# A decode kernel that streams 544 MB: seven small weight loads in one descriptor a partition instead of two, and a reordered last head

## The chip, the cores and the metric

The kernel runs on one core of one Trainium2 chip. The metric is the device time in microseconds (us), the median of several executions. A second number is used throughout: the *span*, from the first to the last of the program's own instructions in the trace. The device time is above the span, and how much above is called *outside* below.

The engines of the core have short names in the profile; in this kernel PE does matmuls (PEld is its loading of weights), DVE does elementwise work and reductions, ACT applies functions such as exp, POOL does next to nothing (0.9 us busy), and SP issues the loads. A load is described by *descriptors*, and here each descriptor became one *packet* (the change takes 7 x 128 descriptors away, and the page after has exactly 896 packets less), moved by one of the core's sixteen DMA engines. A load has *landed* when its last packet has arrived. The *granted clock* is the share of full speed that PE is allowed at a time; the clock records of the traces before and after hold only 1.00 and 0.50.

A ratio is the mean time of one kernel's fast runs over that of the kernel before in the same rounds, so it is not quite the ratio of the medians quoted beside it.

## The reference, cut to what matters

One token is decoded: 16 query heads share 8 key/value heads ("pairs" of query heads), with 65,536 cached tokens of 256 values each. The output is projected by `wo`, mixed with a small MLP branch and gated.

```
def _A_ref(x, k_cache, v_cache, wq, wo):          # Hq, Hkv, Sk, Dh = 16, 8, 65536, 256;  D = 448
    q = (x @ wq) ...
    scores = jnp.einsum("bhqd,bhkd->bhqk", q, k) * (Dh ** -0.5)
    p = _softmax(scores, axis=-1)
    o = jnp.einsum("bhqk,bhkd->bhqd", p, v)
    return o.reshape(B, Sq, Hq * Dh) @ wo
# return g * a + (1 - g) * b
```

K and V together are 537 MB. They must be read once, so the kernel is a stream with some arithmetic beside it. (The cut leaves out transposes and the repeating of K and V.)

## The kernel before

SP issues every load on one queue: for each of 32 steps a K load and a V load of 8 MB each (128 partitions of 64 KB), and at the first step of each of the eight pairs 448 KB of `wo`. The `wo` slice of a pair has 512 rows of 448 bf16 values. Partition p gets rows 2p and 2p+1 of each of the two query heads, which are two runs of 1792 bytes, hence two descriptors a partition:

```
    load(vbuf, A_v_cache, j, 0, NLATE if last else NV, 0, sem_v)
    if last:
        for (n0, n1), sem in zip(pieces, sem_vp):      # pieces = (96,112), (112,124), (124,128)
            load(vbuf, A_v_cache, j, n0, n1, 0, sem)
    if j % PPH == 0:
        g = j // PPH
        if g >= 1:
            eng.wait_ge(s_proj, g)
        eng.dma_start(wo_sb[:, :, :], A_wo[g * REP * DH:(g + 1) * REP * DH, :].rearrange(
                          "(h p j) n -> p h (j n)", h=REP, j=2)).then_inc(sem_wo, 16)
```

PE multiplies values by weights in *column groups*: four tokens share one bank, each in its own 32 rows. At a head change DVE copies the bank to `accs`, two selecting matmuls (`by_d`) bring the sums into columns, DVE divides by the denominators, and PE projects with `wo`. In the last head the last tokens are instead multiplied directly into columns (`late_values`), so that the copy (0.46 us in the timeline below) and the selecting matmuls (0.61 us) need not come after the last byte:

```
    some(0, NLATE).then_inc(s_early, 1)                # column groups, tokens 0 to 95
    ... else branch of the last step:
    def tail():
        late_values(*pieces[0])                        # tokens 96..111, directly
        pe.wait_ge(s_cp, H)                            # DVE has copied accs
        by_d(sps[:, 0, 0:2 * REP])                     # two selecting matmuls
        late_values(pieces[1][0], NV).then_inc(s_late, 1)   # tokens 112..127, directly
        pe.wait_ge(sem_wo, 16 * H)
        pe.wait_ge(s_oTn, H)
        project()
```

The softmax here doesn't subtract the row's maximum and nothing guards it: scores larger than these inputs give would overflow.

Of the kernel before, what the change touches and what calls it, by code (L numbers as in the profile page):

```python
# [8 lines left out]
ALU = mybir.AluOpType  # L9
# [3 lines left out]
def bass_gated_mix__gqa_block_cached__mixer_token_mlp__decode_kernel(  # L13
# [15 lines left out]
    f32 = mybir.dt.float32  # L29

    H = A_k_cache.shape[1]
    T = A_k_cache.shape[2]
    DH = A_k_cache.shape[3]
    DM = A_x.shape[-1]
    HQ = A_wq.shape[1] // DH
    REP = HQ // H
    F = B_w1.shape[1]
    FT = F // 128
    P = 128
# [11 lines left out]
    NV = BODY * NT  # L51
# [9 lines left out]



    NLATE = 96
    pieces = [(NLATE, 112), (112, 124), (124, NV)]


    NCG = 4
# [22 lines left out]
    with ctx:  # L91
        def sb(shape, dt, name):
            return ctx.enter_context(nc.sbuf_tensor(name, shape, dt))
# [17 lines left out]

        wo_sb = sb([P, REP, 2 * DM], bf16, "wo_sb")

        early = vbuf[:, :, :].rearrange("p n d -> p (n d)")
        early_f = vbuf_f[:, :, :].rearrange("p n d -> p (n d)")
        wq_a = early[:, 0:WF * NQ].rearrange("p (j n) -> p j n", j=WF)
# [26 lines left out]
        zrow = sb([1, NACC], bf16, "zrow")  # L143
        rden = sb([P, REP], f32, "rden")
        densum = sb([P, REP], f32, "densum")
        b2_b = sb([1, 1], bf16, "b2_b")
        stat = sb([1, 8], f32, "stat")
        statb = sb([1, 8], bf16, "statb")
# [65 lines left out]
        @block.sync  # L214
        def _(eng):
            eng.dma_start(wq_a.rearrange("p j n -> p (j n)"),  # L216
                          A_wq[0:WF * P, :].rearrange("(p j) n -> p (j n)", p=P)).then_inc(sem_wq, 16)
            eng.dma_start(wq_b, A_wq[WF * P:DM, :].rearrange("r (a n) -> (r a) n", a=2)  # L218
                          ).then_inc(sem_wq, 16)
            def load(dst, cache, j, n0, n1, at, sem):  # L220
                eng.dma_start(dst[:, at + n0:at + n1, :].rearrange("p n d -> p (n d)"), src(cache, j, n0, n1)  # L221
                              ).then_inc(sem, 16)

            for j in range(NP):
                last = j == NP - 1
                if j >= 1:
                    eng.wait_ge(sem_tr[NB - 1], BODY * (j - 1) + DC)
                if j == 0:
                    load(kring, A_k_cache, j, HV, NV, 0, sem_k)
                    load(kring, A_k_cache, j, 0, HV, 0, sem_kb)  # L230
                elif last:
                    load(kring, A_k_cache, j, 0, HV, HV, sem_k)
                    load(kring, A_k_cache, j, HV, NV, HV, sem_kb)
                else:
                    load(kring, A_k_cache, j, 0, NV, HV * (j % 2), sem_k)
                if j == 0:
                    eng.wait_ge(s_q, 1)
                    eng.wait_ge(s_hb, 1)
                else:
                    eng.wait_ge(sem_pv, j)  # L240
                load(vbuf, A_v_cache, j, 0, NLATE if last else NV, 0, sem_v)
                if last:
                    for (n0, n1), sem in zip(pieces, sem_vp):
                        load(vbuf, A_v_cache, j, n0, n1, 0, sem)
                if j % PPH == 0:
                    g = j // PPH
                    if g >= 1:
                        eng.wait_ge(s_proj, g)
                    eng.dma_start(wo_sb[:, :, :],
                                  A_wo[g * REP * DH:(g + 1) * REP * DH, :].rearrange(  # L250
                                      "(h p j) n -> p h (j n)", h=REP, j=2)).then_inc(sem_wo, 16)
            eng.wait_ge(s_fin, 1)
            eng.dma_start(out_ap, out_g[0:P:P // NCG, :]).then_inc(sem_out, 16)
            eng.wait_ge(sem_out, 16)
# [13 lines left out]
        def _(pe):  # L268
# [54 lines left out]
            def values(j, c0, u16):  # L323
                with pe.If(j == NP - 1):
                    spin(8)
                pe.wait_ge(sem_exp, c0 + (BODY + 2))
                for r in range(BODY):
                    pe.matmul(acc[:, DENC:SELC], ones_sq[:, :], pT[:, r, :],  # L328
                              start=False, stop=(r == BODY - 1), skip_group_check=True)

                def some(n0, n1):
                    pe.wait_ge(sem_v, u16)
                    for n in range(n0, n1):
                        r, nt = divmod(n, NT)
                        o = 32 * (n % 4)
                        ins = pe.matmul(acc[o:o + REP, 0:DH], pT[:, r, 2 * nt:2 * nt + 2], vbuf[:, n, :],  # L336
                                        start=False, stop=False, skip_group_check=True)
                    return ins

                some(0, NLATE).then_inc(s_early, 1)  # L340
                with pe.If(j < NP - 1):
                    some(NLATE, NV).then_inc(sem_pv, 1)
                with pe.Else():
                    tail()

            def piece_wait(n):
# [4 lines left out]
            def late_values(n0, n1):  # L351
                for n in range(n0, n1):
                    r, nt = divmod(n, NT)
                    piece_wait(n)
                    for dj in range(2):
                        ins = pe.matmul(sps[:, 0, dj * REP:(dj + 1) * REP], vbuf[:, n, dj:DH:2],  # L356
                                        pT[:, r, 2 * nt:2 * nt + 2], start=(n == NLATE and dj == 0),
                                        stop=(n == NV - 1), skip_group_check=True)
                return ins

            def by_d(dst):
                for dj in range(2):
                    ins = pe.matmul(dst[:, dj * REP:(dj + 1) * REP], accs[:, dj:DH:2], sel[:, :],
                                    start=False, stop=True, skip_group_check=True)
                return ins

            def clear(bank):
                pe.matmul(bank, ones_sq[0:1, :], zrow[0:1, 0:bank.shape[-1]], start=True, stop=True,
                          skip_group_check=True)

            def project():
                for hh in range(REP):
                    for dj in range(2):
                        j = dj * REP + hh
                        for q in range(NCG):
                            ins = pe.matmul(prj[32 * q:32 * q + 1, 0:WG], oTn[:, j:j + 1],  # L376
                                            wo_sb[:, hh, dj * DM + q * WG:dj * DM + (q + 1) * WG],
                                            start=False, stop=True, skip_group_check=True)
                ins.then_inc(s_proj, 1)


            def tail():
                late_values(*pieces[0])
                pe.wait_ge(s_cp, H)
                by_d(sps[:, 0, 0:2 * REP])
                late_values(pieces[1][0], NV).then_inc(s_late, 1)
                pe.wait_ge(sem_wo, 16 * H)
                pe.wait_ge(s_oTn, H)
                project()

            pe.sem_inc(sem_qk, 2)
            pe.wait_ge(sem_ident, 1)
# [34 lines left out]
            with nc.Fori(0, H, 1, engines=on, head_slot={pe.engine: 0}) as g:  # L427
                with nc.Fori(0, PPH, 1, engines=on, head_slot={pe.engine: 0}) as m:
                    j = pe.snap(g * PPH + m, min_val=0, max_val=NP - 1)
                    c0 = pe.snap(j * BODY, min_val=0, max_val=NC)  # L430
                    u16 = pe.snap(j * 16 + 16, min_val=16, max_val=16 * NP)
                    keys(c0, j, u16, pe.snap(x2_reg, min_val=0, max_val=NV))
                    values(j, c0, u16)
                    with pe.If(j < FT):
                        pe.wait_ge(s_pb, j + 1)
                        for q in range(NCG):
                            pe.matmul(prj[32 * q:32 * q + 1, WG:2 * WG], w2cur[:, :],
                                      gu[:, q * WG:(q + 1) * WG], start=False, stop=True, skip_group_check=True)
                    pe.reg_sub(x2_reg, NV, x2_reg)
                with pe.If(g < H - 1):  # L440
                    pe.wait_ge(s_cp, g + 1)
                    clear(acc[:, 0:NACC])
                    by_d(acc[:, SELC:NACC]).then_inc(s_sel, 1)
                    pe.wait_ge(sem_wo, pe.snap(g * 16 + 16, min_val=16, max_val=16 * H))
                    pe.wait_ge(s_oTn, g + 1)
                    project()

        @block.vector
        def _(vec):
# [107 lines left out]
            def finish_head(g):  # L557
                take(vec.snap(g * PPH + PPH, min_val=PPH, max_val=NP))
                vec.tensor_copy(qcur[:, :, :], qT[:, :, bass.ds(g * REP + REP, REP)])
                vec.drain()  # L560
                vec.wait_ge(s_sel, g + 1)
                by_head(acc[:, SELC:NACC])

            vec.wait_ge(s_q, 1)
            vec.tensor_copy(qT[:, :, :].rearrange("p a b -> p (a b)"), sps[:, 1, 0:2 * HQ])
# [23 lines left out]
            with nc.Fori(NC - NCPH, NC, BODY, engines=on) as c0:  # L589
                for k in range(BODY):  # L590
                    evacuate(k, c0 + k)
            take(NP, s_early)
            vec.wait_ge(s_late, 1)
            by_head(sps[:, 0, 0:2 * REP])
            vec.wait_ge(s_proj, H)
# [71 lines left out]
```

## Time and profile before

| | before |
|---|---|
| median of 3 runs | 1267.58 us (1267.54 to 1267.93) |
| span of the profiled run | 1265.7 us |
| busy: PE, ACT, DVE | 72%, 42%, 33% |
| DMA queue, share of 16 engines' span | 99.6% |
| last V piece has landed (trace's semaphore record) | 1262.00 us after the start |

First some lines of the page of the kernel before: the span, the busy time of the engines (with shares and instruction counts), the busy share of the DMA engines in 40 slices, their packets, the one data queue, and the shares of the chain of work that ended last.

```profile
span 1265.7 us, 38663 instructions
...
PE 911.9 (72%) x17040; PEld 861.1 (68%) x17041; DVE 418.2 (33%) x741; ACT 537.2 (42%) x786; POOL 0.9 (0%) x7
...
DMA  9999999999999999999999999999999999999998
...
DMA packets 12509, 544.39 MB, mean 430 GB/s; under 512 B 1360, under 2 KB 3410, under 8 KB 3794
...
q1 hardware_dynamic: 12408, 544.22, 99.6%
...
DMA 70%; PE 29%; issue 1%; SPq 0%; DVE 0%; ACT 0%; ACTq 0%
```

The DMA row is at 9 (90% or more) from the first slice to the last but one, and the queue's packets fill 99.6% of what sixteen engines have. So the queue does not run dry, and bytes and packets decide when the last byte lands. That the chain gives 29% to PE only says that a load is issued when PE has freed a buffer (the queue waited 31 times for the PE line L336 below, and 31 times for PE's reading of K); mostly 7 to 12 us of other loads are still queued at that moment (an estimate: K loads land 27.8 us after their issue and V loads 29.8 us in the median, and successive landings are 19.4 us apart, which leaves 8 and 10 us).

The queue's own waits before, by the line of the kernel that waits, what it waited for, the time in total, the number of waits and the longest:

```profile
SPq L221 <- PE acc L336: 531.3, 31, 23.7
...
SPq L249 <- PE prj L376: 13.0, 7, 1.9
```

The second line is the wait for the projection ahead of a `wo` load. It happens seven times and lasts 1.9 us at most.

The end of the timeline before. The columns are start in us, time in us, engine, line, operation, tiles, shapes and count; in brackets the idle time before and what ended it.

```profile
1257.11 2.79 PE L336 MATMUL acc<-vbuf,pT 128*2 128x256 bf16 x96 [0.72 <-DMA vbuf<-in_A_v_cache_dram]
...
1259.83 0.96 PE L356 MATMUL sps<-pT,vbuf 128*128 128x2 bf16 x32
1259.95 0.46 DVE L543 COPY accs<-acc 128x288 f32<-128x288 f32 x1 [6.80 <-PE acc L336]
...
1260.65 0.61 PE L363 MATMUL sps<-sel,accs 128*128 128x2 f32 x4
...
1261.45 0.95 PE L356 MATMUL sps<-pT,vbuf 128*128 128x2 bf16 x32 [0.19 <-DMA vbuf<-in_A_v_cache_dram]
1262.44 0.16 DVE L554 TENSOR_TENSOR oTn<-sps,rden 128x4 bf16<-128x4 f32 x1 [1.51 <-PE sps L356]
...
1262.75 0.54 PE L376 MATMUL prj<-wo_sb,oTn 128*1 128x112 bf16 x16 [0.35 <-DVE oTn L554]
1263.34 0.33 DVE L596 SCALAR_TENSOR_TENSOR out_g<-prj,bcast,run_g 128x112 bf16<-128x112 f32 x1 [0.74 <-PE prj L376]
```

The 96 tokens in column groups are followed by tokens 96 to 111 directly (L356), the copy on DVE (L543), the two selecting matmuls (L363), the last 16 tokens (L356 again, at 1261.45), the division (L554), the projection (L376), and the output step (L596). The 12-token piece landed at 1261.40 and the 4-token piece at 1262.00.

One more line, the window over the projection before: window, its length, then busy us (and count) of PE, weight loads, DVE, ACT and POOL, the granted clock of PE, the DMA share and GB/s.

```profile
1262.60:1263.30 0.70, 0.54 (x16) 0.31 (x16) 0.00 (x1) 0.00 (x0) 0.00 (x0) 0.50 0.00 0
```

The clock granted to PE was 0.50 there. The clock's records say that it fell at 1262.58 us. The records in this trace stand on a grid of 3.41 us.

### The profile page before, as it was taken

The numbers are of one execution on the slowest core, as the hardware profiler recorded it, in microseconds if no ns is written. First come the engines' busy times: TensorE is split into PE (matmuls) and PEld (weight loads), VectorE is DVE, ScalarE is ACT, GpSimd is POOL, SyncE is SP. The second block draws the span as 40 slices with busy tenths as digits, with TensorE's granted clock in tenths as the row PEclk, the third lists the DMA queues.
The fourth block names the chain that finished last, engine by engine and source line by source line (L and its number), as shares of the span: only waits on it lengthen the run. The fifth ranks groups of instructions, "written<-read, shape, count | busy, mean of one in ns | idle before, by whom it ended". The sixth has DMA issues, their size and how long they took to land.

```text
span 1265.7 us, 38663 instructions
## 1 busy us (share of the span) xinstructions
PE 911.9 (72%) x17040; PEld 861.1 (68%) x17041; DVE 418.2 (33%) x741; ACT 537.2 (42%) x786; POOL 0.9 (0%) x7
## 2 busy tenths in 40 slices
PE   2876668766778666787666876768867678666698
PEld 2766668766677666686665876657766578665687
DVE  2433334333344233343222332223322233331233
ACT  1543335533355333454333553335543245432455
POOL 0000000000000000000000000000000000000000
PEclk9888789788898788888788888789887788887989
DMA  9999999999999999999999999999999999999998
GB/s 412 428 429 437 431 435 433 433 431 437 431 433 435 431 433 437 429 435 435 431 433 433 433 435 435 431 427 439 433 435 435 425 433 439 433 435 429 431 426 353
DMA packets 12509, 544.39 MB, mean 430 GB/s; under 512 B 1360, under 2 KB 3410, under 8 KB 3794
## 3 DMA queue, kind: packets, MB, share of 16 engines
q1 hardware_dynamic: 12408, 544.22, 99.6%
q8 instruction: 8, 0.13, 0.0%
q10 hardware_dynamic: 90, 0.01, 0.0%
q14 instruction: 3, 0.02, 0.0%
HBM read 544.22 MB, written 0.00 MB: 430 GB/s over the span
## 4 chain that ended last, share of the span: by engine, by line
DMA 70%; PE 29%; issue 1%; SPq 0%; DVE 0%; ACT 0%; ACTq 0%
DMA kring<-in_A_k_cache_dram 68%; PE kst L284 24%; PE sps L304 4%; DMA vbuf<-in_A_v_cache_dram 2%; PE acc L336 0%; PE sps L356 0%; SPq L221 0%; PE prj L376 0%; SPq L218 0%; SPq L216 0%; PE acc L328 0%; DVE out_g L596 0%; ACT pT L621 0%; DVE oTn L554 0%; ACTq L621 0%
## 5 line engine op out<-in xcount | busy, mean ns | idle before, releaser
L284 PE MATMUL kst<-ident,kring 128*128 128x128 f32 x4096 | 560.9, 298 | 313.2 <-DMA kring<-in_A_k_cache_dram 301.1
L632 ACT ACTIVATE ktT<-kst 128x1024 bf16<-128x1024 bf16 x512 | 499.4, 1021 | 669.1 <-PE kst L284 668.8
L284 PEld LDWEIGHTS kst<-ident,kring 128*128 128x128 f32 x4096 | 511.1, 155 | 322.9 <-issue 320.7
L538 DVE COPY ktT<-kst 128x1024 bf16<-128x1024 bf16 x512 | 354.3, 692 | 771.5 <-PE kst L284 748.2
L304 PEld LDWEIGHTS sps<-qcur,ktT 128*128 128x128 bf16 x8192 | 237.7, 96 | 4.9 <-issue 2.4
L304 PE MATMUL sps<-qcur,ktT 128*128 128x2 bf16 x8192 | 236.7, 163 | 2.0 <-issue 2.0
L336 PE MATMUL acc<-vbuf,pT 128*2 128x256 bf16 x4064 | 145.1, 312 | 2.3 <-issue 1.6
L336 PEld LDWEIGHTS acc<-vbuf,pT 128*2 128x2 bf16 x4064 | 107.3, 95 | 31.6 <-issue 2.1
L621 ACT ACTIVATE pT<-sps 128x32 f32 x256 | 52.2, 204 | 17.0 <-PE sps L304 17.0
L328 PE MATMUL acc<-pT,ones_sq 128*128 128x32 bf16 x256 | 11.7, 178 | 12.2 <-ACT pT L621 12.2
L328 PEld LDWEIGHTS acc<-pT,ones_sq 128*128 128x128 bf16 x256 | 8.6, 96 | 15.2 <-ACT pT L621 14.9
L543 DVE COPY accs<-acc 128x288 f32<-128x288 f32 x8 | 3.7, 458 | 39.6 <-PE acc L336 39.6
L638 ACT ACTIVATE z_b<-z_b 128x448 bf16<-128x448 bf16 x14 | 8.1, 576 | 20.5 <-DVE z_b L525 20.5
L400 PE MATMUL acc<-vbuf 42*128 42x42 bf16 x1 | 0.2, 214 | 8.3 <-DMA b_b<-in_B_b_dram 8.3
L517 DVE TENSOR_TENSOR wtmp<-u_b 128x448 bf16<-128x448 bf16 x14 | 5.5, 393 | 1.0
L523 DVE TENSOR_TENSOR z_b<-u_b,wtmp 128x448 bf16<-128x448 bf16 x14 | 5.5, 393 | 1.0
L519 DVE TENSOR_TENSOR z_b<-wtmp,u_b 128x448 bf16<-128x448 bf16 x14 | 5.5, 393 | 1.0
L531 DVE TENSOR_TENSOR gu<-wtmp,z_b 128x448 bf16<-128x448 bf16 x14 | 5.5, 393 | 1.0
L400 PEld LDWEIGHTS acc<-vbuf 42*128 42x128 bf16 x1 | 0.1, 98 | 8.4 <-DMA b_b<-in_B_b_dram 8.4
L529 DVE TENSOR_SCALAR z_b<-z_b 128x448 bf16<-128x448 bf16 x14 | 3.9, 277 | 5.7 <-ACT z_b L638 5.7
L515 DVE TENSOR_SCALAR u_b<-wtmp,params 128x448 bf16<-128x448 bf16 x14 | 4.7, 337 | 2.6 <-issue 2.6
L513 DVE TENSOR_SCALAR wtmp<-hbT,params 128x448 bf16<-128x448 bf16 x14 | 4.7, 336 | 2.6 <-issue 2.6
(84 smaller groups left out, 76.2 us busy)
## 6 DMA issues: line engine op xcount, KB each, us to landing
kring<-in_A_k_cache_dram SPq DMA_DIRECT2D x4, 4096.0 KB, 24.3
vbuf<-in_A_v_cache_dram SPq DMA_DIRECT2D x1, 6144.0 KB, 24.3
wo_sb<-in_A_wo_dram SPq DMA_DIRECT2D x8, 448.0 KB, 28.6
vbuf<-in_A_wq_dram SPq DMA_DIRECT2D x1, 3072.0 KB, 10.4
vbuf<-in_A_v_cache_dram SPq DMA_DIRECT2D x1, 1024.0 KB, 26.0
vbuf<-in_A_v_cache_dram SPq DMA_DIRECT2D x1, 768.0 KB, 27.5
vbuf<-in_A_wq_dram SPq DMA_DIRECT2D x1, 512.0 KB, 11.2
vbuf<-in_A_v_cache_dram SPq DMA_DIRECT2D x31, 29.8
```

The costliest lines, as they stand in the source:

```text
L284: ins = pe.transpose(kst[:, b, i * P:(i + 1) * P], kring_f[:, at + NT * (k % DC) + 4 * b + i, :], ident[:, :])
L304: ins = pe.matmul(sps[:, par, 2 * nt:2 * nt + 2], ktT[:, par, b, ntl * DH + dj:(ntl + 1) * DH:2], qcur[:, dj, :], start=(dj == 0), stop=(d ...
L328: pe.matmul(acc[:, DENC:SELC], ones_sq[:, :], pT[:, r, :], start=False, stop=(r == BODY - 1), skip_group_check=True)
L336: ins = pe.matmul(acc[o:o + REP, 0:DH], pT[:, r, 2 * nt:2 * nt + 2], vbuf[:, n, :], start=False, stop=False, skip_group_check=True)
L517: vec.tensor_tensor(W, U, U, op=ALU.mult)
L519: vec.tensor_tensor(Z, W, U, op=ALU.mult)
L523: vec.tensor_tensor(Z, U, W, op=ALU.add)
L531: vec.tensor_tensor(gu[:, :], W, Z, op=ALU.mult).then_inc(s_pb, 1)
L538: vec.tensor_copy(ktT[:, k % KTB, b, :], kst_b[:, b, :]).then_inc(sem_ev[b], 1)
L621: act.activation(pT[:, bass.ds(p0 + k % DC, 1), :].rearrange("p o n -> p (o n)"), sps[:, k % 2, 0:2 * NT], AF.Exp, scale=scale).then_inc(s ...
L632: act.activation(ktT[:, k % KTB, b, :], kst_b[:, b, :], AF.Copy).then_inc(sem_ev[b], 1)
L638: act.activation(z_b[:, :], z_b[:, :], AF.Tanh).then_inc(s_tanh, 1)
```

## The change

It has two halves. For pairs 0 to 6 partition p now gets four consecutive rows (4p to 4p+3) of `wo`, one run of 3584 bytes, so one descriptor. The sums must then be brought to other partitions: eight selecting matmuls of 64 columns (`by_row`) instead of two of 128, and DVE divides by a per-partition column that two small copies make. In the last head tokens 96 to 111 go through column groups, only 16 tokens are multiplied directly, and one dummy matmul (`spin`), whose result nobody reads, runs on PE before the projection. The diff, cut to its core:

```diff
-    NLATE = 96
-    pieces = [(NLATE, 112), (112, 124), (124, NV)]
+    NFIRST = 96
+    NLATE = 112
+    pieces = [(NFIRST, NLATE), (NLATE, 124), (124, NV)]
 ...
-                    eng.dma_start(wo_sb[:, :, :], ... "(h p j) n -> p h (j n)", h=REP, j=2)
+                    if g < H - 1:
+                        eng.dma_start(wo_rows, w.rearrange("(p i) n -> p (i n)", i=2 * REP)).then_inc(sem_wo, 16)
+                    else:
+                        (the load as before)
 ...
-                some(0, NLATE).then_inc(s_early, 1)
+                some(0, NFIRST)
 ...             (last step)
+                    some(NFIRST, NLATE, last=True).then_inc(s_early, 1)
                     tail()
 ...
+            def by_row(dst):
+                for hh in range(REP):
+                    for i in range(2 * REP):
+                        ins = pe.matmul(dst[hh * HP:(hh + 1) * HP, i:i + 1], accs[:, i:DH:2 * REP],
+                                        sel[:, hh:hh + 1], start=False, stop=True, skip_group_check=True)
+                return ins
 ...
             def tail():
-                late_values(*pieces[0])
                 pe.wait_ge(s_cp, H)
                 by_d(sps[:, 0, 0:2 * REP])
-                late_values(pieces[1][0], NV).then_inc(s_late, 1)
+                late_values(NLATE, NV).then_inc(s_late, 1)
+                spin(1)
 ...             (head change, DVE)
+                for hh in range(REP):
+                    h = slice(hh * HP, (hh + 1) * HP)
+                    vec.tensor_copy(rrow[h, :], rden[h, hh:hh + 1])
+                vec.drain()
                 vec.wait_ge(s_sel, g + 1)
-                by_head(acc[:, SELC:NACC])
+                vec.tensor_scalar(oTn[:, :], acc[:, SELC:NACC], rrow[:, :], None, op0=ALU.mult).then_inc(s_oTn, 1)
```

More of the change, by code (lines that the diff above doesn't have):

```diff
@@ L112, in bass_gated_mix__gqa_block_cached__mixer_token_mlp__decode_kernel @@
         wo_sb = sb([P, REP, 2 * DM], bf16, "wo_sb")
+        wo_rows = wo_sb[:, :, :].rearrange("p h n -> p (h n)")
+        HP = P // REP
+        assert 2 * REP * HP == DH
         early = vbuf[:, :, :].rearrange("p n d -> p (n d)")
@@ L145, in bass_gated_mix__gqa_block_cached__mixer_token_mlp__decode_kernel @@
         densum = sb([P, REP], f32, "densum")
+        rrow = sb([P, 1], f32, "rrow")
         b2_b = sb([1, 1], bf16, "b2_b")
@@ L240, in _ @@
                     eng.wait_ge(sem_pv, j)
-                load(vbuf, A_v_cache, j, 0, NLATE if last else NV, 0, sem_v)
+                load(vbuf, A_v_cache, j, 0, NFIRST if last else NV, 0, sem_v)
                 if last:
@@ L248, in _ @@
                         eng.wait_ge(s_proj, g)
-                    eng.dma_start(wo_sb[:, :, :],
-                                  A_wo[g * REP * DH:(g + 1) * REP * DH, :].rearrange(
-                                      "(h p j) n -> p h (j n)", h=REP, j=2)).then_inc(sem_wo, 16)
+                    w = A_wo[g * REP * DH:(g + 1) * REP * DH, :]
+                    if g < H - 1:
+                        eng.dma_start(wo_rows, w.rearrange("(p i) n -> p (i n)", i=2 * REP)).then_inc(sem_wo, 16)
+                    else:
+                        eng.dma_start(wo_sb[:, :, :], w.rearrange("(h p j) n -> p h (j n)", h=REP, j=2)
+                                      ).then_inc(sem_wo, 16)
             eng.wait_ge(s_fin, 1)
@@ L329, in values, with some @@
                               start=False, stop=(r == BODY - 1), skip_group_check=True)
-                def some(n0, n1):
-                    pe.wait_ge(sem_v, u16)
+                def some(n0, n1, last=False):
+                    if last:
+                        piece_wait(n0)
+                    else:
+                        pe.wait_ge(sem_v, u16)
                     for n in range(n0, n1):
@@ L338, in some @@
                     return ins
-                some(0, NLATE).then_inc(s_early, 1)
+                some(0, NFIRST)
                 with pe.If(j < NP - 1):
-                    some(NLATE, NV).then_inc(sem_pv, 1)
+                    some(NFIRST, NV).then_inc(sem_pv, 1)
                 with pe.Else():
+                    some(NFIRST, NLATE, last=True).then_inc(s_early, 1)
                     tail()
@@ L356, in late_values @@
                         ins = pe.matmul(sps[:, 0, dj * REP:(dj + 1) * REP], vbuf[:, n, dj:DH:2],
-                                        pT[:, r, 2 * nt:2 * nt + 2], start=(n == NLATE and dj == 0),
+                                        pT[:, r, 2 * nt:2 * nt + 2], start=False,
                                         stop=(n == NV - 1), skip_group_check=True)
@@ L363, in by_d @@
                     ins = pe.matmul(dst[:, dj * REP:(dj + 1) * REP], accs[:, dj:DH:2], sel[:, :],
-                                    start=False, stop=True, skip_group_check=True)
+                                    start=(dj == 0), stop=True, skip_group_check=True)
+                return ins
[4 more added lines that the diff above has]
+                                        sel[:, hh:hh + 1], start=False, stop=True, skip_group_check=True)
                 return ins
@@ L369, in clear, with project @@
                           skip_group_check=True)
-            def project():
-                for hh in range(REP):
-                    for dj in range(2):
-                        j = dj * REP + hh
-                        for q in range(NCG):
-                            ins = pe.matmul(prj[32 * q:32 * q + 1, 0:WG], oTn[:, j:j + 1],
-                                            wo_sb[:, hh, dj * DM + q * WG:dj * DM + (q + 1) * WG],
-                                            start=False, stop=True, skip_group_check=True)
+            def project(cols):
+                for i, j in enumerate(cols):
+                    for q in range(NCG):
+                        ins = pe.matmul(prj[32 * q:32 * q + 1, 0:WG], oTn[:, j:j + 1],
+                                        wo_rows[:, i * DM + q * WG:i * DM + (q + 1) * WG],
+                                        start=False, stop=True, skip_group_check=True)
                 ins.then_inc(s_proj, 1)
             def tail():
-                late_values(*pieces[0])
                 pe.wait_ge(s_cp, H)
                 by_d(sps[:, 0, 0:2 * REP])
-                late_values(pieces[1][0], NV).then_inc(s_late, 1)
+                late_values(NLATE, NV).then_inc(s_late, 1)
+                spin(1)
                 pe.wait_ge(sem_wo, 16 * H)
                 pe.wait_ge(s_oTn, H)
-                project()
+                project([dj * REP + hh for hh in range(REP) for dj in range(2)])
             pe.sem_inc(sem_qk, 2)
@@ L442, in _ @@
                     clear(acc[:, 0:NACC])
-                    by_d(acc[:, SELC:NACC]).then_inc(s_sel, 1)
+                    by_row(acc[:, SELC:NACC]).then_inc(s_sel, 1)
                     pe.wait_ge(sem_wo, pe.snap(g * 16 + 16, min_val=16, max_val=16 * H))
                     pe.wait_ge(s_oTn, g + 1)
-                    project()
+                    project(range(2 * REP))
         @block.vector
@@ L591, in _ @@
                     evacuate(k, c0 + k)
-            take(NP, s_early)
+            take(1, s_early)
             vec.wait_ge(s_late, 1)
```

## The prediction

> **What bounds the kernel.** The page's DMA row is at 9 in every slice but the last, the queue view puts one queue at 99.6% of sixteen engines' span. PE is busy 72%, ACT 42%, DVE 33%. By the queue's issues a cache load lands 24 to 35 us after its issue, where its own bytes take 19.4 us (successive landings): 7 to 10 us of work are always queued ahead. So bytes and packets set the time up to the last landing; then comes a serial tail, 4.3 us from the landing of the 12-token V piece (1261.40; the 4-token piece: 1262.00) to the end.
>
> **Part 1, wo in one descriptor.** A wo load is now 256 packets of 1792 B, sixteen an engine; the packet records give 77 ns each, 1.23 us a load. After: 128 packets of 3584 B. Packets of 2048, 4096 and 6144 B took 84, 159 and 237 ns: 37 ns per KB plus about 8 ns a packet, so 3584 B should take 140 ns (an estimate): 1.12 us a load, 0.11 us less, 0.75 us for seven. [...] With the queue always full, all of it should reach the end.
>
> **Its price.** At seven head changes two fp32 matmuls become eight; the timeline shows 0.12 us a pass, two passes each: up to 1.4 us more on PE (an estimate). After the projection PE waits 7.0 to 8.5 us for the next K, so this is absorbed. The queue's wait for the projection before wo, now 1.9 us, grows to at most 3.5, with 27 us of work queued: nothing lost.
>
> **Part 2, the tail.** Tokens 96 to 111 move from 32 direct matmuls (25 ns apart) to 16 in column groups (26 ns apart). The DVE copy (0.46 us), which started at 1259.95, now waits for them, 0.6 us longer, so the two selecting matmuls (0.47 us) end near 1261.5 on the old trace's clock instead of 1261.1, while the matmuls of the 12-token piece started at 1261.445. What was hidden under a landing becomes about 0.1 us of critical wait.
>
> **The spin.** The granted clock falls to 0.5 at 1262.58, and the projection took 0.57 us; at a head change at clock 1.0 it took 0.40. The spin (0.24 us, as the eight before it) fits into the 0.48 us in which PE waits for DVE and costs nothing. [...] the clock records stand on a grid of 3.41 us[...]. Worth 0 to 0.17 us. The tail nets about zero.
>
> **Prediction.** 1267.58 - 0.75 + 0 to 0.1: 1266.9 us, 8 in 10 between 1266.3 and 1267.5. Faster by over 2%: 0.01; within 2%: 0.98; slower: 0.01.
>
> **What would show it.** 896 packets of 3584 B at 140 ns; wo loads of 1.12 us; the last V pieces landing 0.75 us earlier; selecting matmuls ending after the 12-token piece's landing; PE's wait for K at a head's start shorter by 1.4 us, not gone; a tail of 4.2 to 4.4 us.
>
> **What would make it wrong.** The packets not scaling so, or their saving not reaching the end; a clock at 0.5 already in the late matmuls; chips differing by over 0.3 us.

What decides whether a spin can hold the clock was not shown. 1267.58 - 0.75 + 0 to 0.1 came to 1266.8 to 1266.9 us, the 0.75 worked out from the packets' measured times, and the 0 to 0.1 an estimate of what the tail nets (about 0.1 us of wait, against 0 to 0.17 us for the spin, from the projection's 0.57 and 0.40 us).

## The result, and the profile after

The changed kernel took 1267.32 us (median of 6 runs, 1267.27 to 1267.76) against 1267.51 us of the kernel before (6 runs, 1267.39 to 1267.93). The ratio is 0.9999, with a 95% interval from 0.9986 to 1.0012: the same. The time lies inside the predicted range, but of the predicted 0.68 us (1267.58 to 1266.9) only 0.19 us came, and that is no more than the scatter of either kernel's runs. Where the rest went is the question.

The same lines of the page after:

```profile
span 1265.2 us, 38823 instructions
...
PE 913.4 (72%) x17110; PEld 864.6 (68%) x17110; DVE 420.5 (33%) x755; ACT 537.4 (42%) x786; POOL 0.9 (0%) x7
...
DMA  9999999999999999999999999999999999999998
...
DMA packets 11613, 544.39 MB, mean 430 GB/s; under 512 B 1360, under 2 KB 1618, under 8 KB 2898
...
q1 hardware_dynamic: 11512, 544.22, 99.6%
...
DMA 70%; PE 29%; issue 1%; DVE 0%; SPq 0%; ACT 0%; ACTq 0%
```

The packets fell by exactly 896 (12509 to 11613), with the same bytes. The span fell from 1265.745 to 1265.165 us (unrounded), so by 0.58 us, three times what the device time shows. The queue's waits after:

```profile
SPq L229 <- PE acc L350: 525.9, 31, 23.5
...
SPq L259 <- PE prj L397: 17.4, 6, 3.0
...
SPq L261 <- PE prj L397: 2.8, 1, 2.8
```

The wait for the projection grew from 1.9 to at most 3.0 us. The end of the timeline after:

```profile
1256.67 3.23 PE L350 MATMUL acc<-vbuf,pT 128*2 128x256 bf16 x112 [0.73 <-DMA vbuf<-in_A_v_cache_dram]
1259.95 0.46 DVE L564 COPY accs<-acc 128x288 f32<-128x288 f32 x1 [7.24 <-PE acc L350]
...
1260.46 0.63 PE L378 MATMUL sps<-sel,accs 128*128 128x2 f32 x4 [0.57 <-DVE accs L564]
...
1261.00 1.00 PE L371 MATMUL sps<-pT,vbuf 128*128 128x2 bf16 x32
...
1261.86 0.38 PE L331 MATMUL kst<-ktT,ones_sq 128*128 128x512 bf16 x1
1262.03 0.16 DVE L575 TENSOR_TENSOR oTn<-sps,rden 128x4 bf16<-128x4 f32 x1 [1.11 <-PE sps L371]
...
1262.35 0.37 PE L397 MATMUL prj<-wo_sb,oTn 128*1 128x112 bf16 x16
1262.77 0.33 DVE L621 SCALAR_TENSOR_TENSOR out_g<-prj,bcast,run_g 128x112 bf16<-128x112 f32 x1 [0.57 <-PE prj L397]
```

All of it stands about 0.4 us earlier. The copy on DVE, which now waits for 112 tokens, starts at the same 1259.95 as before. The gap of 0.22 us that PE had between its column groups and the next matmuls is gone, because the next tokens are now part of the same stretch. The projection takes 0.37 us instead of 0.54.

Two things from the traces' semaphore records set this out. "Landed" is when the last V piece is complete, "tail" the time from there to the end of the span, "outside" the device time of the profiled run less its span.

| | landed | tail | span | device time of that run | outside |
|---|---|---|---|---|---|
| before | 1262.00 | 3.75 | 1265.75 | 1267.55 | 1.81 |
| after | 1261.60 | 3.57 | 1265.17 | 1267.33 | 2.16 |

So the landing gained 0.40, the tail 0.18, and about 0.36 us were lost where no instruction of the program runs. Following the landings of all loads in the two traces, the difference grows like a staircase: 0.06 us before the second `wo` load, 0.14 after it, then 0.18, 0.25, 0.31, 0.38, 0.44 after the next five, and no step at the eighth load, whose shape was not changed. A single pair of profiles gives the last landing only roughly: it lies between 1261.82 and 1262.26 us in the seven profiles with the old loads and between 1261.54 and 1261.65 in the five with the new ones, e6 and e7 left out. The means differ by 0.40 us.

### The profile page after: what moved, and what is told of

The parts are those of the page before. It is cut to its first block, busy times and chain, and to the rows that moved or that the text cites. A ratio compares the mean times of both kernels' runs of the same rounds, so it can differ in the third digit from the quotient of the medians.

```text
span 1265.2 us, 38823 instructions
## 1 busy us (share of the span) xinstructions
PE 913.4 (72%) x17110; PEld 864.6 (68%) x17110; DVE 420.5 (33%) x755; ACT 537.4 (42%) x786; POOL 0.9 (0%) x7
## 2 busy tenths in 40 slices
DMA packets 11613, 544.39 MB, mean 430 GB/s; under 512 B 1360, under 2 KB 1618, under 8 KB 2898
## 3 DMA queue, kind: packets, MB, share of 16 engines
q1 hardware_dynamic: 11512, 544.22, 99.6%
## 4 chain that ended last, share of the span: by engine, by line
DMA 70%; PE 29%; issue 1%; DVE 0%; SPq 0%; ACT 0%; ACTq 0%
DMA kring<-in_A_k_cache_dram 68%; PE kst L295 24%; PE sps L315 4%; DMA vbuf<-in_A_v_cache_dram 2%; PE acc L350 1%; PE sps L371 0%; PE sps L378 0%; DVE accs L564 0%; SPq L226 0%; PE prj L397 0%; SPq L224 0%; PE acc L339 0%; DVE out_g L621 0%; PE kst L331 0%; ACT pT L646 0%
## 5 line engine op out<-in xcount | busy, mean ns | idle before, releaser
L350 PE MATMUL acc<-vbuf,pT 128*2 128x256 bf16 x4080 | 140.3, 305 | 2.6 <-issue 1.8
L386 PEld LDWEIGHTS acc<-sel,accs 128*64 128x64 f32 x112 | 10.8, 214 | 0.9
L386 PE MATMUL acc<-sel,accs 128*64 128x1 f32 x112 | 11.4, 261 | 0.0
```

The lines of the kernel that those rows point to most:

```text
L350: ins = pe.matmul(acc[o:o + REP, 0:DH], pT[:, r, 2 * nt:2 * nt + 2], vbuf[:, n, :], start=False, stop=False, skip_group_check=True)
L386: ins = pe.matmul(dst[hh * HP:(hh + 1) * HP, i:i + 1], accs[:, i:DH:2 * REP], sel[:, hh:hh + 1], start=False, stop=True, skip_group_check= ...
```

## The experiments

Twelve kernels were run (no run e10 is on record). Each comes with the kernel before on the same chip. First the theories. *A*: saved packets are worth what the landings show, and the faster projection is only a matter of whether it runs before or after a fall of the granted clock. *B*: the spin holds the clock. And for the 0.36 us outside the span: an accident of one profile, or something in the change.

### e0_before: the kernel before, unchanged

> The unchanged kernel, run as if it were an experiment, to learn how far its span (first to last profiled instruction) differs from run to run and how far the reported time lies above the span. In the two profiles so far that distance is 1.85 us before and 2.12 to 2.19 us after, so 0.58 us less span became 0.19 us less time. If the distance belongs to the kernel, the kernel before shows 1.8 to 1.9 us in every run here; if the one profile of before was an outlier, it shows 2.1 to 2.2 us and spans of about 1265.3 to 1265.4 us. Theory on the clock: the grid of clock records falls where it fell (a drop at 1262.58 us after the start) in this run too; the rival has it anywhere within 3.4 us.

It took 1267.48 us against 1267.66 of the other runs of the very same kernel in the same rounds. That is a difference of 0.18 us between equal kernels, as large as the one measured for the change: medians of a few runs do not resolve it. Its distance to the span was 1.80 us, so that is a property of the kernel and not an accident. The window over the projection in this run:

```profile
1262.60:1263.30 0.70, 0.37 (x16) 0.22 (x16) 0.13 (x2) 0.00 (x0) 0.00 (x0) 1.00 0.00 0
```

The clock was 1.00 and PE took 0.37 us, with the old tail and no spin. Its clock record falls at 1264.97 instead of 1262.58, so the half of theory A that had the fall at a fixed time is wrong. The tail from the last landing was 3.57 us, the same as after the change.

### e1_wo, e2_tail, e3_nospin: the halves apart, and the change without its spin

e1 is the changed kernel with the tail of the kernel before:

```diff
-                pe.wait_ge(s_cp, H)
-                by_d(sps[:, 0, 0:2 * REP])
-                late_values(NLATE, NV).then_inc(s_late, 1)
-                spin(1)
+                late_values(*pieces[0])
+                pe.wait_ge(s_cp, H)
+                by_d(sps[:, 0, 0:2 * REP])
+                late_values(pieces[1][0], NV).then_inc(s_late, 1)
```

> The wo half of the change alone, with the old tail and no spin. Theory A (saved packets, and a fixed clock boundary): a staircase of 0.06 to 0.07 us earlier at each wo load, so the last V pieces land 0.40 to 0.45 us earlier; the projection then runs before the drop at 1262.58 us and takes 0.40 us instead of 0.57; span 0.5 to 0.6 us shorter than the kernel before in the first profile, so as fast as the changed kernel. Theory B (the spin holds the clock): same landings, but the projection still takes 0.57 us, and the kernel is 0.17 us slower than the changed one.

e2 is the changed kernel with the `wo` loads and head changes of the kernel before:

```diff
-                    if g < H - 1:
-                        eng.dma_start(wo_rows, w.rearrange("(p i) n -> p (i n)", i=2 * REP)) ...
+                    eng.dma_start(wo_sb[:, :, :], ... "(h p j) n -> p h (j n)", h=REP, j=2) ...
-                    by_row(acc[:, SELC:NACC]).then_inc(s_sel, 1)
+                    by_d(acc[:, SELC:NACC]).then_inc(s_sel, 1)
```

> The tail half alone: 112 tokens through column groups, 16 directly, spin before the projection, wo loads as before. Theory A: landings as in the kernel before, so the projection begins after the drop at 1262.58 us and takes 0.57 us in spite of the spin; time within 0.1 us of the kernel before. Theory B: the spin keeps the clock, the projection takes 0.40 us, and the span is 0.17 us shorter than the kernel before.

e3 is the changed kernel with one line less:

```diff
                 late_values(NLATE, NV).then_inc(s_late, 1)
-                spin(1)
```

> The changed kernel without its spin. Theory A: the projection takes 0.40 us all the same, time within 0.05 us of the changed kernel. Theory B: the projection takes 0.57 us, time 0.17 us above the changed kernel.

| run | median, of before in the same rounds | landed | tail | projection | outside | clock falls at |
|---|---|---|---|---|---|---|
| e1_wo | 1267.45, 1267.66 | 1261.65 | 3.56 | 0.40 | 2.16 | 1263.32 |
| e2_tail | 1267.39, 1267.66 | 1261.95 | 3.57 | 0.40 | 1.80 | 1265.42 |
| e3_nospin | 1267.46, 1267.66 | 1261.55 | 3.57 | 0.40 | 2.16 | 1265.28 |

(The projection is from the first weight load to the last matmul's end; it was 0.57 in the first profile of the kernel before.) The window over the projection in e2, which has the spin and lands late:

```profile
1262.60:1263.30 0.70, 0.37 (x16) 0.22 (x16) 0.18 (x1) 0.00 (x0) 0.00 (x0) 1.00 0.00 0
```

Everywhere but in that first profile the projection took 0.40 to 0.41 us, with the spin (e2, after) and without it (e0, e1, e3). Theory B falls: no run shows the spin doing anything, and in the profile after the change the clock fell at 1262.58, only 0.34 us after the spin had ended. The time from the last landing to the end is 3.56 to 3.57 us with the old tail, the new tail, and the new tail without spin, so the whole tail half is worth nothing. The times agree: against the kernel before in the same rounds the means of e1 (old tail), of e3 and of the changed kernel (new tail) are lower by 0.15, 0.18 and 0.15 us. The 0.18 us that the tail seemed to gain was a fall of the granted clock to 0.50 (at 1262.58) just ahead of the projection (from 1262.72) in one profile of the kernel before.

What is left is the `wo` half: it lands earlier, and it alone brings the 2.16.

### e4_dma and e5_rows: the load's shape and the added instructions apart

e4 is the kernel before with only the new load; e5 has all the new work on PE and DVE but the old load. Both meet rows of `wo` with the wrong outputs. (The comparison with the reference passed them all the same, as it did e8 and e9, which are wrong too; the attention's part of the output is too small for it to see this. Whether the changed kernel and e11 below compute the right thing therefore rests on reading their code.)

```diff
 e4, against the kernel before:
-                    eng.dma_start(wo_sb[:, :, :], ... "(h p j) n -> p h (j n)", h=REP, j=2)
+                    if g < H - 1:
+                        eng.dma_start(wo_sb as rows, w.rearrange("(p i) n -> p (i n)", i=4))
 e5, against e1_wo:
-                    (the new load)
+                    (the load of the kernel before)
```

> The kernel before with only the shape of the wo loads 0 to 6 changed, the head change computed as before: wrong on purpose (rows of wo meet the wrong outputs). So far the reported time lies 1.80 us above the span where wo is loaded the old way (three profiles) and 2.16 us where the new wo half is in (three profiles), which takes back 0.36 us of what the span gains. Theory P (the added instructions cause it): 1.80 us here, span 0.4 us shorter, median 0.4 us under the kernel before. Theory Q (the load's shape causes it): 2.16 us here, median about 0.1 us under the kernel before. In both the last V piece lands 0.40 to 0.45 us earlier.

> The kernel before with only the computing of the new wo half (eight selecting matmuls, two DVE copies and another last DVE step at each head change), wo loaded the old way: wrong on purpose. Theory P: span as the kernel before within 0.15 us, time 2.16 us above the span, so 0.36 us over the kernel before. Theory Q: 1.80 us above the span, time as the kernel before. In both no landing moves, if the longer head change is absorbed in the wait for K.

e4 took 1267.02 us against 1267.44 (ratio 0.9997, 0.9983 to 1.0010), e5 1267.81 against 1267.44 (1.0004, 0.9990 to 1.0017). The distances to the span were 1.79 and 2.16 us. Theory P holds: the load's shape gives the gain, and the added instructions take most of it back, outside the span (the two means are 0.43 us under and 0.39 us over the kernel before). The page of e4 begins:

```profile
span 1265.1 us, 38664 instructions
```

### e6_two and e7_one: sixty-two more loads in either shape

To measure the packets clear of noise, the kernel before got two dead `wo` loads a step (steps 0 to 30), in two descriptors a partition or in one:

```diff
+                if not last:
+                    for i in range(2):
+                        if j >= 1:
+                            eng.wait_ge(sem_wd[i], 16 * j)
+                        w = A_wo[(j % H) * REP * DH:(j % H + 1) * REP * DH, :]
+                        e6: eng.dma_start(wd[i][:, :, :], w.rearrange("(h p j) n -> p h (j n)", h=REP, j=2)) ...
+                        e7: eng.dma_start(wd[i] as rows, w.rearrange("(p i) n -> p (i n)", i=4)) ...
```

> The kernel before with two more wo loads of 448 KB per pair for pairs 0 to 30 (62 in all, into tiles that nobody reads), each in 256 packets of 1792 B. Result correct. By the packet records at 1.23 us a load 76 us more; by the landings (1.19 us between the landing of V and of wo) 74 us more: 1341 to 1344 us.

> The same 62 loads, each in 128 packets of 3584 B. Theory A (8 ns for each of 8 packets saved on an engine, 0.063 us a load): 3.9 us faster than with two descriptors a partition. Rival, the prediction's 0.11 us a load: 6.8 us. Rival, the packet records' 0.083 us a load: 5.1 us.

The packets and the dead loads of e6 (KB each, median us to landing):

```profile
DMA packets 29373, 572.83 MB, mean 427 GB/s; under 512 B 2352, under 2 KB 20274, under 8 KB 20658
...
wd<-in_A_wo_dram SPq DMA_DIRECT2D x62, 448.0 KB, 33.3
```

and of e7:

```profile
DMA packets 21437, 572.83 MB, mean 429 GB/s; under 512 B 2352, under 2 KB 4402, under 8 KB 12722
...
wd<-in_A_wo_dram SPq DMA_DIRECT2D x62, 448.0 KB, 33.0
```

They took 1342.20 and 1337.88 us (4 runs each, 1342.07 to 1342.43 and 1337.75 to 1338.04). The difference of 4.32 us over 62 loads is 0.070 us a load, or, if the 128 packets saved are 8 on each of 16 engines, 8.7 ns a packet. (Such an even share fits the loads before: sixteen packets of 77.1 ns are 1.23 us, and `wo` landed 1.19 us after V.) That lies between theory A (3.9 us expected) and the records (5.1 us), nearer to A, and far under the prediction's 6.8. e6 itself, 74.8 us above the kernel before, fell where it was expected, so what a load costs reaches the end time. Both distances to the span were 1.84 to 1.85 us.

### e8_pe and e9_dve: whose instructions

```diff
 e8, against e5_rows: DVE as in the kernel before (by_head, no copies)
-                    vec.tensor_copy(rrow[h, :], rden[h, hh:hh + 1])
 e9, against e5_rows: PE as in the kernel before
-                    by_row(acc[:, SELC:NACC]).then_inc(s_sel, 1)
+                    by_d(acc[:, SELC:NACC]).then_inc(s_sel, 1)
```

> The kernel before with only the eight selecting matmuls in place of two at a head change on PE; DVE's program and the wo loads as before (wrong on purpose). The run with all the added instructions and the old loads stood 2.16 us above its span, the kernel before 1.80. If PE's added code costs the 0.36 us outside the span: 2.16 here, median 0.35 us over the kernel before. If DVE's does: 1.80, time as the kernel before. If each has a share: between. Landings as the kernel before in all.

> The kernel before with only DVE's part of the new head change: two copies into a column, a drain, and a multiply by that column in place of the multiply by head (wrong on purpose; PE and the loads as before). If DVE's added code costs the 0.36 us outside the span: 2.16 us above the span, median 0.35 us over the kernel before. If PE's does: 1.80, time as the kernel before.

e8 took 1267.43 us against 1267.45, with 1.80 us outside the span: six more matmuls at each head change cost nothing that shows. e9 took 1268.02 against 1267.45, with 2.16 us outside. It is DVE's part. The median is 0.2 us further up than that explains; in its profile the last piece landed at 1262.26, 0.15 us later than in any other kernel with the old loads, and the spans of all its four runs are high (1265.8 to 1266.0). Why is open. The page of e9 begins:

```profile
span 1265.8 us, 38685 instructions
```

### e11_fold and e12_dead: a short DVE program, and a long one that is not executed

By now two explanations were left: that DVE executes more at head changes, or that its program is longer. The programs as built have 206 DVE instructions in the kernel before (and in e2, e4, e8), 209 in the changed kernel (and in e1, e3, e5, e9). (The number depends on what is counted as an instruction; the differences do not.) e11 is a correct kernel with the new loads and 205: it multiplies the reciprocal into the selecting column, so that `by_row` gives finished values, and it joins two DVE steps on the row of the MLP branch. It keeps the old tail. e12 is the kernel before with the two copies and the drain in a branch that is never taken.

```diff
 e11, against e1_wo:
                 vec.reciprocal(rden[:, :], densum[:, :])
                 vec.drain()
+                if head:
+                    vec.tensor_tensor(selr[:, :], sel[:, :], rden[:, :], op=ALU.mult).then_inc(s_cp, 1)
 ...             (by_row reads selr instead of sel)
-                for hh in range(REP):
-                    h = slice(hh * HP, (hh + 1) * HP)
-                    vec.tensor_copy(rrow[h, :], rden[h, hh:hh + 1])
-                vec.drain()
-                vec.tensor_scalar(oTn[:, :], acc[:, SELC:NACC], rrow[:, :], None, op0=ALU.mult).then_inc(s_oTn, 1)
+                vec.tensor_copy(oTn[:, :], acc[:, SELC:NACC]).then_inc(s_oTn, 1)
-            vec.tensor_scalar(brow, brow1, bcast[:, 2:3], None, op0=ALU.add)
-            vec.drain()
-            vec.tensor_scalar(run_g[:, :], brow, bcast[:, 1:2], None, op0=ALU.mult)
+            vec.tensor_scalar(run_g[:, :], brow1, bcast[:, 2:3], bcast[:, 1:2], op0=ALU.add, op1=ALU.mult)
 e12, against the kernel before:
+                with vec.If(g == H):
+                    for hh in range(REP):
+                        vec.tensor_copy(rrow[h, :], rden[h, hh:hh + 1])
+                    vec.drain()
```

> A correct kernel that keeps the wo loads in one descriptor and DVE's program short: the reciprocal is multiplied into the selecting column (one DVE instruction in place of two copies, a drain and a multiply by column), and two DVE steps of the row that the gate adds are made one; old tail, no spin. DVE's program has 205 instructions; it has 206 in the kernel before and 209 in all kernels that stood 2.16 us above their span. If the 0.36 us belong to the length of DVE's program: 1.80 us above the span, span 1265.1 to 1265.2 us, median 0.40 to 0.45 us under the kernel before and 0.35 us under the changed kernel. If they belong to what is executed there (any new DVE work at head changes): 2.16 us, and no gain over the changed kernel.

> The kernel before with the two DVE copies and the drain in a branch that is never taken (211 DVE instructions in the program, no new work done but the branch). If the program's length costs the 0.36 us: 2.16 us above the span, median 0.35 us over the kernel before. If executing them does: 1.80 us, time as the kernel before.

e11 took 1266.98 us (5 runs, 1266.73 to 1267.12) against 1267.50, ratio 0.9996 (0.9982 to 1.0009), with 1.80 us outside the span. It is the fastest kernel that computes the right thing: 0.52 us of median under the kernel before, where the changed kernel is 0.19 under it (the two were not run in the same rounds). From its page:

```profile
span 1265.1 us, 38837 instructions
...
DMA packets 11613, 544.39 MB, mean 430 GB/s; under 512 B 1360, under 2 KB 1618, under 8 KB 2898
```

e12 took 1267.84 us against 1267.50 (1.0003, 0.9988 to 1.0018), with 2.21 us outside, though it executes nothing new but a branch. Its page begins:

```profile
span 1265.4 us, 38671 instructions
```

So what costs is that these instructions stand in DVE's program, not that they are executed. Their number, the length of the program, is the simplest reading, and the table is headed by it. But every long program here holds the same two copies and drain at the same place, so that any other three instructions would do the same is not shown. All kernels sorted by the two causes, each with the mean of its runs less the mean of the kernel before in the same rounds:

| | DVE program short (205, 206): 1.79 to 1.81 us outside | DVE program long (209, 211): 2.16 to 2.21 us outside |
|---|---|---|
| `wo` in two descriptors | e0 -0.06, e2 -0.20, e8 0.00 | e5 +0.39, e9 +0.61, e12 +0.32 |
| `wo` in one descriptor | e4 -0.43, e11 -0.56 | after -0.15, e1 -0.15, e3 -0.18 |

On average the rows differ by 0.4 us (short) and 0.6 us (long), the columns by 0.5 us (two descriptors) and 0.3 us (one). No two fields overlap, except that the reordered tail alone (e2) falls among the changed kernels. No single comparison here is clear of its own interval at this size.

The record settles it better than this table, since it holds the span of every run, to 0.1 us, and not only of the profiled ones. The time less the span is 1.75 to 1.87 us in all 66 runs with a short DVE program (34 of them runs of the kernel before) and 2.12 to 2.22 us in all 29 with a long one. And the mean span, against the kernel before in the same rounds, is 0.42 to 0.58 us shorter in e1, e3, e4 and e11, which have the new loads, and between 0.22 us shorter and 0.25 us longer in the six kernels with the old ones. So each cause moves its own part of the time, and there is no overlap in either.

Open is *why* this costs 0.36 us outside the span. No view of the profile shows that part, but the kept traces hold semaphore updates after the span, and they say a little more. In every kernel a semaphore that the program does not use is stepped on after the program's end, the last time 1.92 us after it (1.96 in e6 and e7). In e12, and there alone, one of these steps comes 0.51 us after the step before it instead of 0.10, and the last is at 2.33: the 0.41 us of e12 lies there, after the program has ended. In the five profiles with 209 instructions all these steps stand where they stand in the kernel before, so their 0.36 us lies elsewhere outside the span. Within the span the packets of the two queues of kind `instruction` are as many in e12 as in the kernel before (8 and 3). What causes it no run shows, and programs between 206 and 209 instructions were not tried.

## Why the prediction was right or wrong

The time, 1267.32 us, is within 1266.3 to 1267.5, and "within 2%" was right. Point by point:

- **"Bytes and packets set the time up to the last landing"**: right. In every profile the time from the last landing to the end was 3.56 to 3.57 us (3.69 in e6 and e7), except the one with the low clock; everything that varied inside the span was the landing.
- **"0.11 us less a load, 0.75 us for seven"**: the mechanism was right, the size wrong, and this is the term that failed first. The estimate subtracted a value on the fitted line (140 ns) from twice the mean of the records (2 x 77 ns), 14 ns a pair. Both from the line would have been 2 x 74 - 140, that is 8 ns: the fixed part of one packet on that line (84, 159 and 237 ns for 2048, 4096 and 6144 B), which is all that merging two packets saves by it. The records after say 143.5 ns on average (2 x 77.1 less that is 10.7 ns a pair, 0.085 us a load). The landings say less: from the second K load to the last half of the last one, six changed `wo` loads further on, the five kernels with the new loads took 1169.19 us on average and the seven with the old ones 1169.55, which is 0.060 us a load, 7.5 ns a packet; e6 and e7 say 0.070. The spacing of the loads around a `wo` load does shorten by 0.081 us (20.542 to 20.461 us from the V load ahead of it to the K load behind it), nearly what the records say, but a part is lost again: the V load just ahead lands 0.03 to 0.04 us later at the second and the sixth `wo` load (not at the others), and the four loads from there to the next take together some 0.01 us longer. Why was not found out. Seven loads make 0.42 us in place of 0.75; the first profile's landings show 0.40 to 0.44.
- **"Up to 1.4 us more on PE, absorbed in the wait for K"**: right. The eight selecting matmuls end 1.0 us later than the two did, PE's idle time before the next K after a head change is shorter by 1.0 to 1.3 us in six of seven (the other is 0.5 us longer, as the step before it ended 1.9 us earlier), and 6.4 us or more remain. e8 shows that this part costs nothing. The queue's wait grew to 3.0 us, under the 3.5 given.
- **What the prediction did not have**: that code which costs nothing in the trace can cost outside of it. Its price list named PE's matmuls and the queue's wait and no instruction of DVE. Inside the span DVE's new work is absorbed, but with it in DVE's program the device time lay 0.36 us further above the span (e5, e9; 0.41 in e12). This took back most of the 0.42 us, and weighs as much as the 0.33 us by which the saving was overestimated.
- **Luck**: the upper end of the range, 1267.5 us, lies at the median of the kernel before in the same rounds (1267.51), so almost no gain at all would have fallen into it. The time did so with about a quarter of the expected gain, after two errors that the prediction had not seen.
- **"About 0.1 us of critical wait from the selecting matmuls"**: wrong. In the trace after, the matmuls of the 12-token piece begin at 1261.00, 0.04 us after its landing at 1260.955, as before. Set against the landings the copy came 0.44 us later, not 0.6: the sixteen tokens take 0.44 us, and the 0.22 us gap that PE had before the directly multiplied tokens vanished when the column groups became one stretch. (By the modelled ends of the trace the last selecting matmul ends at 1261.09, after the landing, as the prediction said, but PE issues the next ones before that.)
- **The spin, "0 to 0.17 us"**: the range held, at zero. The 0.57 us of the projection before was one profile's accident (e0, the same kernel, took 0.40); no run shows the spin moving it. The clock did not fall at a fixed time: in six profiles its last fall came at 1262.58, 1262.58, 1263.32, 1264.97, 1265.28 and 1265.42 us after the start.

## What to carry to other kernels

On this queue, which was always full (99.6%), merging two descriptors saved about the fixed part of one packet (7.5 to 8.7 ns) and no more: take both sides of such an estimate from the same fit, and check the size on the landings of later loads rather than on the sum of packet records. Compare the device time with the span in every run: what DVE's added instructions cost outside the span (0.36 us) is shown by no view of the trace, and here it ate most of a gain that the trace showed plainly. And before a tail is reworked, look at the time from the last landing to the end in several profiles, since one fall of the granted clock to 0.50 looked like 0.18 us of work here.
